# An order written out for every engine is replaced by another, with twelve small dummy matmuls near its start

## The chip, the cores and the metric

One core of one Trainium2 chip runs the kernel. Five engines work side by side on that core, each through its own list of instructions in order: TensorE (PE, matmuls), VectorE (DVE), ScalarE (ACT), GpSimd (POOL) and SyncE (SP, which here only issues transfers). The metric is device microseconds (us) of one execution.

## What is computed

Attention whose mask comes from hashes, then a channel mix with squared relu. Cut to its core, with batch 4, 8 heads, 768 positions and head size 64:

```
bucket(x) = sum_k 2**k * ((x @ proj)[k] > 0)                  # 6 bits
mask      = bucket(q)[:, None] == bucket(k)[None, :]
attn      = softmax(where(mask, q @ k.T / 8, -1e9))           # per batch and head
x         = attn @ v, heads side by side                      # 4 x 768 x 512
xk, xr    = mu_k*x + (1-mu_k)*x_prev, mu_r*x + (1-mu_r)*x_prev # x_prev: one position back
out       = sigmoid(xr @ w_r) * (relu(xk @ w_k)**2 @ w_v)      # d_ff 1024
```

## The kernel before

The heads are worked two at a time: 16 pairs, n = 0 to 15, four pairs to a batch. Each pair goes through a chain of steps; the names are those that the planner's keys use, with the line that issues them.

- Loads (`ldq`, `ldv`, L452 to L470, SP) bring q, k and v of a pair. `hi` (L540, for pairs 0 to 2 L612 and L614) and `lo` (L543, L617; DVE) split q and k into two halves of 16 bits.
- Transposes: for pairs 0 to 2 by PE (`t`, L631) with a copy out (`evt`, L635, DVE or ACT), for the rest by a DMA (`tr`, SP). A step ends in a digit that stands for the head of the pair: `lo0q1` is pair 0, q, head 1.
- Hash bits: 24 small matmuls (`bits`, L571), one DVE step (`bx`, L575) and two or four small DMAs (`row`, L595, SP) write the bits as extra rows beside q and k, so that the score matmul adds the mask. For pair 0 the bits go straight (`b`, L653, and `beb`, L659 on ACT or L661 on DVE).
- Scores: nine steps for each pair, 1024 columns each, `sc` (L704, PE) then `exp` (L708, ACT). A score step takes two PSUM banks of six (banks 0 to 5, slots 0, 2, 4) and holds them until its `exp` has read them.
- Values: `va`, `vsum`, `vsumb`, `vsumc` (L485 to L499, POOL or DVE), `oo` (L732, L737, PE), `rc` and `ob` (L747 to L754, DVE), `ot` and `xt` (L790 to L796) or a DMA transpose, `xs` and `xj` (L772 to L777, a small shift).
- After the four pairs of a batch, the channel mix of that batch: `df`, `xk`, `xr` (DVE), 16 steps `kp` (L855, PE) with `relu` (L860 on ACT, L862 on DVE) and a squaring `sq` (L865, DVE), and six steps each of `r` (L880, PE), `tanh` (L883, ACT), `v` (L895, PE), `os` (L902, DVE) and a store (L906). The channel mix of one batch lies among the scores of the next; the last one has nothing behind it.

Nothing of the order is decided when the kernel is built. `add` and `add_on` collect about 1400 steps. Three tables say the rest: `WHERE` gives an engine to each step that has a choice, `SLOT` a PSUM bank to each matmul step, and `ORDER` is the sequence in which `schedule` hands the steps out. Each engine works off its own steps in that sequence, and a step that waits holds up all that stand behind it on its engine. The dummy matmuls on a zeroed buffer (`warm`, L370, seven of 128x512) take part in the order as any other step; a second set (L373) stands in the code with a count of 0. The weights come by DMA and are cast by the steps `wc` (L434 to L436).

Of the kernel before, what the change touches and what calls it, by code (L numbers as in the profile page):

```python
# [36 lines left out]
def R(kind, n):  # L37
# [195 lines left out]
def kernel(  # L233
# [13 lines left out]
    nc = tc.nc  # L247
# [5 lines left out]
    P = 128  # L253
# [11 lines left out]
    NWARM2 = 0  # L265
# [90 lines left out]
    def sm(name):  # L356
        b_ = plan.slot[name]
        return ps_all[:, b_ * 512 : (b_ + 1) * 512]
# [604 lines left out]
```

## Time and profile before

| | |
|---|---|
| median of three runs | 250.05 us (248.19, 250.05, 250.88) |
| the profiled execution | 248.25 us, of which 246.5 us is the span from its first instruction to its last |
| outside the span | 1.75 us |
| granted TensorE clock | 1.000 |
| PE instructions | 2643 matmuls, 2643 weight loads |

A line of the profile's groups reads: line, engine, operation, what it writes and reads, shapes, count, then busy us and mean ns of one, then the idle time of the engine before such instructions and what ended it. In the sequences a number behind a line is its start in us from the span's begin and the next its length. The length of a matmul has its way through the array in it; from one matmul's start to the next is the time that it takes of PE.

### The profile page before, as it was taken

What the parts mean: (1) busy time and instruction counts of PE and PEld (TensorE: products, weight loads), DVE (VectorE), ACT (ScalarE), POOL (GpSimd) and SP (SyncE); (2) the same over time, 40 slices, a digit from 0 to 9 for tenths busy, and PEclk for the clock granted to TensorE, in tenths of its full rate; (3) what the DMA queues carried; (4) which work ended last, traced back from release to release, by engine and by line L of the source; (5) the groups of instructions that cost most, each with busy time, mean ns of one, the idle gap of its engine ahead of it and who ended that gap; (6) DMA issues with size and microseconds to landing.
All of it is one profiled execution on the core that took longest, in us unless ns stands there. A gap on an engine that the chain in (4) does not pass through costs nothing.

```text
span 246.5 us, 6589 instructions
## 1 busy us (share of the span) xinstructions
PE 236.3 (96%) x2643; PEld 148.2 (60%) x2643; DVE 193.7 (79%) x451; ACT 178.0 (72%) x224; POOL 52.5 (21%) x104
## 2 busy tenths in 40 slices
PE   6989899999999999999999999999999999999994
PEld 2456578876766656556566567755676554455443
DVE  3899977879999797879999788889569986575313
ACT  3698979999999988669878999998873241334320
POOL 5132841348114221204221113013010000000000
PEclk9999999999999999999999999999999999999999
DMA  6986998899689899996989797695211031321033
GB/s 188 338 289 180 199 274 172 299 225 164 195 272 236 277 187 292 215 264 176 220 277 176 207 292 150 171 199 126 88 32 47 12 107 43 128 86 44 0 128 128
DMA packets 71161, 43.77 MB, mean 178 GB/s; under 512 B 51356, under 2 KB 66140, under 8 KB 71132
## 3 DMA queue, kind: packets, MB, share of 16 engines
q1 hardware_dynamic: 71036, 43.36, 69.7%
q8 instruction: 20, 0.33, 0.5%
q14 instruction: 9, 0.07, 0.1%
q10 hardware_dynamic: 96, 0.01, 0.0%
HBM read 24.12 MB, written 6.29 MB: 123 GB/s over the span
## 4 chain that ended last, share of the span: by engine, by line
PE 76%; DVE 14%; DMA 5%; issue 2%; SPq 1%; ACT 1%; POOL 0%; DVEq 0%
PE ps_all L704 19%; PE ps_all L895 16%; PE ps_all L855 15%; PE ps_all L737 10%; PE ps_all L880 8%; PE ps_all L571 4%; DMA a<-bx 4%; DVE nh L543 3%; DVE nh L540 2%; DVE nh L617 1%; DMA pj<-in_proj_dram 1%; DVE ob L754 1%; SPq L595 1%; DVE a L661 1%; PE ps_all L631 1%
## 5 line engine op out<-in xcount | busy, mean ns | idle before, releaser
L708 ACT ACTIVATE pt<-ps_all 128x1024 bf16<-128x1024 f32 x144 | 138.2, 1044 | 14.6 <-PE ps_all L704 13.3
L704 PE MATMUL ps_all<-a 128*128 128x256 f16 (+3 forms) x408 | 80.4, 316 | 0.9 <-DMA a<-bx 0.8
L855 PE MATMUL ps_all<-xk,wk 128*128 128x384 bf16 x256 | 49.5, 326 | 0.0
L737 PEld LDWEIGHTS <-pt 128*128 128x128 bf16 x1152 | 43.1, 97 | 9.2 <-issue 1.1
L704 PEld LDWEIGHTS <-a 128*128 128x128 f16 x408 | 34.9, 97 | 22.4 <-issue 2.6
L895 PE MATMUL ps_all<-wv,k 128*128 128x512 bf16 (+2 forms) x208 | 46.5, 362 | 0.5 <-DVE ob L754 0.5
L737 PE MATMUL ps_all<-va,pt 128*128 128x65 bf16 x1152 | 45.2, 193 | 0.0
L855 PEld LDWEIGHTS <-wk 128*128 128x128 bf16 x256 | 24.1, 98 | 16.1 <-issue 0.8
L860 ACT ACTIVATE kr<-ps_all 128x384 bf16<-128x384 f32 x37 | 17.7, 494 | 20.3 <-PE ps_all L855 13.5
L895 PEld LDWEIGHTS <-k 128*128 128x128 bf16 x208 | 19.5, 98 | 19.8 <-issue 0.8
L883 ACT ACTIVATE rs<-ps_all 128x512 f32<-128x512 f32 x24 | 14.1, 598 | 22.1 <-PE ps_all L880 17.7
L902 DVE SCALAR_TENSOR_TENSOR os<-rs,ps_all 128x512 f32<-128x512 f32 (+2 forms) x26 | 16.7, 643 | 15.9 <-PE ps_all L895 9.1
L865 DVE TENSOR_TENSOR k<-kr 128x384 bf16<-128x384 bf16 x64 | 23.6, 387 | 5.0 <-ACT kr L860 4.8
L543 DVE SCALAR_TENSOR_TENSOR nh<-nat,nh 128x768 f16<-128x768 f32 x26 | 25.9, 1005 | 0.6 <-issue 0.2
L880 PE MATMUL ps_all<-wr,xr 128*128 128x512 bf16 x96 | 23.7, 379 | 0.0
L862 DVE TENSOR_SCALAR kr<-ps_all 128x384 bf16<-128x384 f32 x27 | 14.9, 552 | 6.8 <-PE ps_all L855 6.1
L754 DVE TENSOR_TENSOR ob<-ps_all,rc 128x384 bf16<-128x384 f32 (+1 forms) x36 | 18.1, 508 | 1.3 <-DMA xt<-ob 0.7
L540 DVE TENSOR_SCALAR nh<-nat 128x768 f16<-128x768 f32 x22 | 15.1, 689 | 0.3 <-DMA nat<-in_k_dram 0.2
L880 PEld LDWEIGHTS <-xr 128*128 128x128 bf16 x96 | 9.0, 98 | 9.5 <-issue 0.2
L571 PE MATMUL ps_all<-a,p0g 128*32 128x256 f16 (+1 forms) x180 | 12.9, 276 | 0.1
L571 PE MATMUL ps_all<-a,p1g 128*32 128x256 f16 (+1 forms) x180 | 12.8, 273 | 0.0
L485 POOL CAST va<-vn 128x768 bf16<-128x768 f32 x7 | 7.7, 1096 | 22.4 <-DMA vn<-in_v_dram 20.8
(93 smaller groups left out, 210.9 us busy)
## 6 DMA issues: line engine op xcount, KB each, us to landing
vn<-in_v_dram SPq DMA_DIRECT2D x16, 384.0 KB
out_dram<-os SPq DMA_DIRECT2D x23, 256.0 KB
nat<-in_q_dram SPq DMA_DIRECT2D x15, 384.0 KB
nat<-in_k_dram SPq DMA_DIRECT2D x15, 384.0 KB
wst<-in_moe_w_k_dram SPq DMA_DIRECT2D x2, 512.0 KB
wst<-in_moe_w_r_dram SPq DMA_DIRECT2D x2, 512.0 KB
wst<-in_moe_w_v_dram SPq DMA_DIRECT2D x2, 512.0 KB
a<-bx SPq DMA_DIRECT2D x48, 9.0 KB
```

The source lines that it names most:

```text
L540: e.tensor_scalar(out=o, in0=x, scalar1=QS, scalar2=None, op0=ALU.mult)
L543: nc.vector.scalar_tensor_tensor(out=nh[:, :, D:P], in0=nat.rearrange("p j (c d) -> p (j c) d", d=D), scalar=QS, in1=nh[:, :, 0:D], op0=AL ...
L571: nc.tensor.matmul(ps[g_ * wid : (g_ + 1) * wid, 0:FW], w_[:, m_ - 1 - x : m_ - 1 - x + wid], a_t[sa][:, i, x % NFOLD * FW : (x % NFOLD + ...
L704: nc.tensor.matmul(ps[:, lo - s * w : hi - s * w], side_a["k"][sa][:, j, jc * P : (jc + 1) * P], side_a["q"][sa][:, j, q0 : q0 + hi - lo], ...
L708: nc.scalar.activation(out=pt_t[sp][:, s * w : (s + 1) * w], in_=ps_all[:, plan.slot[nm] * 512 : plan.slot[nm] * 512 + w], func=AF.Exp, bi ...
L737: nc.tensor.matmul(oo[:, (ic - c0) * 65 : (ic - c0) * 65 + 65], pt_t[sp][:, o : o + P], va_t[sa][:, j, jc, 0 : D + 1], start=(not uc and i ...
L754: nc.vector.tensor_tensor(out=ob_t[so][:, c0:c1, j * D : (j + 1) * D], in0=oo[:, :, 0:D], in1=rc_t[sr][:, 1, c0:c1].unsqueeze(2).to_broadc ...
L855: nc.tensor.matmul(ps[:, 0:HALF], wk_sb[:, d, fc * P : (fc + 1) * P], xk_t[mx[d]][:, h * HALF : (h + 1) * HALF], start=(d == 0), stop=(d = ...
L860: nc.scalar.activation(out=kr_t[sk], in_=sm(nm)[:, 0:HALF], func=AF.Relu, scale=0.5 ** 0.5)
L865: nc.vector.tensor_tensor(out=k2_t[s2][:, h * HALF : (h + 1) * HALF], in0=kr_t[sk], in1=kr_t[sk], op=ALU.mult)
L880: nc.tensor.matmul(sm(nr), xr_t[mx[d]][:, c * P : (c + 1) * P], wr_sb[:, d, :], start=(d == 0), stop=(d == NDC - 1))
L895: nc.tensor.matmul(sm(nv)[:, lo:hi], k2_t[(b * NFC + fc) % NK2][:, c * P : (c + 1) * P], wv_sb[:, fc, lo:hi], start=(fc == 0), stop=(fc == ...
```

## The change

Twelve dummy matmuls of 128x256 (`keep`, L373) are added beside the seven `warm`, and all three tables are new. The dummies have places in the order as all other steps have.

```
-    NWARM2 = 0
+    NKEEP = 12
...
-    for i in range(NWARM2):
-        add("PE", 0.2155, -7.5 + 0.15 * i, lambda: nc.tensor.matmul(sm("warm2"), wz[:, 0:P], wz, start=True, stop=True),
...
+    for i in range(NKEEP):
+        add("PE", 0.109, -7.5 + 0.15 * i, lambda: nc.tensor.matmul(sm("warm2")[:, 0:256], wz[:, 0:P], wz[:, 0:256], start=True, stop=True),
...
 WHERE = {
-    "wc8": "ACT", "wc9": "POOL", "hi0q0": "DVE", "evt0q00": "DVE", ...
+    "wc8": "POOL", "wc9": "DVE", "hi0q0": "DVE", "evt0q00": "ACT", ...
 SLOT = {
-    "warm": 7, "mu": 6, "t0q00": 7, "b0q00": 7, "t0q01": 6, ...
+    "warm": 6, "warm2": 7, "mu": 6, "t0q00": 4, "b0q00": 6, "t0q01": 5, ...
 ORDER = [
...
+    0, 76, 84, 85, 79, 77, 110, 111, 9, 10, 11, 2, 3, 4, 104, 5, 12, 13, 27, 51, 78, 82, 105, 6,
...
```

What changes engine, counted over the new table: nine `relu` go from ACT to DVE in sum (37 on ACT and 27 on DVE become 28 and 36; by batch, ACT has 6, 9, 10, 12 before and 6, 5, 12, 5 after); three `vsum` steps go from POOL to DVE; of 18 `xs`, POOL has 14 before and 6 after (DVE 9, ACT 3); three `xj` go from POOL to DVE; one weight cast goes from ACT to POOL and one from POOL to DVE; one `beb` goes from DVE to ACT; of 14 copies `evt`, ACT has 5 before and 3 after. SP issues the same transfers, in another order.

What the new sequence is at the start, by names and engine (before above, after below):

```
PE   warm*4 t0k10 warm*3 t0q10 b0k10 t0k01 b0q10 t0q01 t0k00 t0q00 b0k01 sc0_5 b0q00 t1q10 b0k00 sc0_7 ...
     keep*3 warm*4 keep*2 warm keep*2 warm t0q01 keep*2 t0q00 keep t0k10 keep warm t0q10 keep b0k10 b0q10 t0k01 b0q00 t1k00 sc0_8 sc0_7 t0k00 b0q01 b0k01 sc0_6 ...
PE   ... bits2 sc1_4 sc1_2 oo0_0*2 sc1_7 sc1_6 oo0_1*2 sc1_0 oo0_0 sc1_1 oo0_1 sc2_1 sc2_7 ot0 sc2_5 mu sc2_6 bits3
     ... bits2 sc1_4 sc1_1 oo0_0 sc1_0 mu oo0_0*2 sc1_6 sc1_7 oo0_1*2 sc1_2 oo0_1 sc2_3 sc2_7 sc2_5 ot0 sc2_1 bits3
DVE  hi0k1 lo0k1 hi0q1 lo0q1 hi0k0 lo0k0 evt0q10 hi0q0 lo0q0 beb0q10 evt0q00 hi1q1 ...
     hi0q0 lo0q0 hi0k1 lo0k1 hi0q1 lo0q1 evt0k10 hi0k0 evt0q10 lo0k0 lo1k0 beb0q10 evt0q01 ...
DVE  ... evt2k10 vsum0 vsum0b hi4k bx2 hi3k lo3 lo4 hi4q lo4 rc0 ob0 rc0 ob0 muv xt0_0
     ... evt2k00 bx2 hi3k lo3 lo4 muv rc0 hi5q hi4k ob0 rc0 ob0 lo4 xt0_0
ACT  ... exp1_4 exp1_2 exp1_7 exp1_6 exp1_0 exp1_1 exp2_1 exp2_7 exp2_6
     ... exp1_4 exp1_1 exp1_0 exp1_6 exp1_7 exp1_2 exp2_3 exp2_5 exp2_7
SP   ldq0k1 ldq0q1 ldq0k0 ldq0q0 ldq1q ldq1k ldq2q ldq2k ldv1 ...
     ldq0q0 ldq0k1 ldq0q1 ldq0k0 ldq1k ldq2q ldq1q ldq2k ldq3q ldv0 ...
```

`mu` is a small matmul that turns the two mix vectors; `muv` is its DVE copy.

More of the change, by code (lines that the diff above doesn't have):

```diff
@@ L371 @@
             r=["wz"], w=["warm"], take=("sm", "warm", 0) if i == 0 else None, give=["warm"] if i == NWARM - 1 else [], name="warm")
-    for i in range(NWARM2):
-        add("PE", 0.2155, -7.5 + 0.15 * i, lambda: nc.tensor.matmul(sm("warm2"), wz[:, 0:P], wz, start=True, stop=True),
-            r=["wz"], w=["warm2"], take=("sm", "warm2", 0) if i == 0 else None, give=["warm2"] if i == NWARM2 - 1 else [], name="keep")
+    for i in range(NKEEP):
+        add("PE", 0.109, -7.5 + 0.15 * i, lambda: nc.tensor.matmul(sm("warm2")[:, 0:256], wz[:, 0:P], wz[:, 0:256], start=True, stop=True),
+            r=["wz"], w=["warm2"], take=("sm", "warm2", 0) if i == 0 else None, give=["warm2"] if i == NKEEP - 1 else [], name="keep")
     add("ACT", 1.5, -9.5, lambda: nc.scalar.activation(out=tb[:, 0:1], in_=tb[:, 1:2], func=AF.Exp), r=["tb"], w=["tb0"], at=0.75, name="table")
```

227 rows, old and new, of tables (ORDER, SLOT, WHERE) are left out of this document.

## The prediction

> **What bounds the kernel now.** I read the page first (busy shares, then the slices), then busy time by stages, then the waits of PE, then the start in order of time on PE, DVE and ACT, because the slices show that PE is short of work only there.
>
> ```profile
> span 246.5 us, 6589 instructions
> PE 236.3 (96%) x2643; PEld 148.2 (60%) x2643; DVE 193.7 (79%) x451; ACT 178.0 (72%) x224; POOL 52.5 (21%) x104
> PE   6989899999999999999999999999999999999994
> DVE  3899977879999797879999788889569986575313
> ACT  3698979999999988669878999998873241334320
> ...
> L708 ACT ACTIVATE pt<-ps_all 128x1024 bf16<-128x1024 f32 x144 | 138.2, 1044 | 14.6 <-PE ps_all L704 13.3
> ...
> L860 ACT ACTIVATE kr<-ps_all 128x384 bf16<-128x384 f32 x37 | 17.7, 494 | 20.3 <-PE ps_all L855 13.5
> ...
> L862 DVE TENSOR_SCALAR kr<-ps_all 128x384 bf16<-128x384 f32 x27 | 14.9, 552 | 6.8 <-PE ps_all L855 6.1
> ...
> L540 DVE TENSOR_SCALAR nh<-nat 128x768 f16<-128x768 f32 x22 | 15.1, 689 | 0.3 <-DMA nat<-in_k_dram 0.2
> ```
> ```profile
> 0.00:32.00 32.00, 27.05 (x275) 16.40 (x275) 25.47 (x48) 24.65 (x32) 13.69 (x43) 1.00 0.85 238
> 32.00:66.00 34.00, 33.34 (x582) 25.67 (x582) 28.95 (x67) 32.57 (x36) 15.30 (x24) 1.00 0.92 224
> 66.00:131.00 65.00, 63.80 (x710) 39.43 (x709) 57.43 (x131) 54.94 (x66) 14.79 (x21) 1.00 0.96 237
> 131.00:186.00 55.00, 55.00 (x708) 35.93 (x709) 44.70 (x116) 48.12 (x57) 8.74 (x16) 1.00 0.73 158
> 186.00:246.50 60.50, 57.17 (x379) 30.79 (x375) 37.18 (x92) 17.71 (x36) 0.00 (x0) 1.00 0.21 73
> ```
>
> The columns after the stretch's length are PE, weight loads, DVE, ACT, POOL, then clock, DMA share and GB/s. PE idles 4.95 us to 32, 0.66 to 66, 1.20 to 131, none to 186, and 3.33 behind its last matmul: 10.14 us. A matmul's length runs into the next, so short gaps are hidden and this is a lower bound. From 32 to 66 ACT is the tight one (32.57 of 34): there is no channel mix yet to fill PE, and the scores wait for their exponentials. From 66 on PE is the bound. So a new order can gain in three places only: the start, ACT's saturation up to 66, and 1.2 us of waits up to 131.
>
> **The start, and its prices.**
>
> ```profile
> PE ps_all L631 <- POOL p L391: 1.2, 1, 1.2
> ...
> PE ps_all L790 <- DVE ob L754: 1.0, 1, 1.0
> PE ps_all L704 <- DMA a<-bx: 0.8, 2, 0.5
> ...
> PE ps_all L895 <- DVE ob L754: 0.5, 1, 0.5
> ```
> ```profile
> 1.19 1.89 PE L370 MATMUL ps_all<-k 128*128 128x512 bf16 x4 [1.19 <-DVE k L367]
> 4.28 0.82 PE L631 MATMUL ps_all<-idh,nh 128*128 128x128 f16 x6 [1.20 <-POOL p L391]
> 4.89 1.49 PE L370 MATMUL ps_all<-k 128*128 128x512 bf16 x3
> 6.17 0.85 PE L631 MATMUL ps_all<-idh,nh 128*128 128x128 f16 x6
> ...
> 11.40 0.51 PE L631 MATMUL ps_all<-idh,nh 128*128 128x128 f16 x6
> ...
> 23.42 1.04 PE L704 MATMUL ps_all<-a 128*128 128x512 f16 x5
> ...
> 29.04 1.05 PE L704 MATMUL ps_all<-a 128*128 128x128 f16 x8 [0.32 <-DMA a<-bx]
> 31.08 0.51 PE L790 MATMUL ps_all<-idb,ob 128*128 128x128 bf16 x6 [1.00 <-DVE ob L754]
> ```
> ```profile
> 3.27 0.36 DVE L614 TENSOR_SCALAR nh<-nat 128x384 f16<-128x384 f32 x1 [2.13 <-DMA nat<-in_k_dram]
> 3.66 0.56 DVE L617 SCALAR_TENSOR_TENSOR nh<-nat,nh 128x384 f16<-128x384 f32 x1
> ...
> 5.91 0.36 DVE L614 TENSOR_SCALAR nh<-nat 128x384 f16<-128x384 f32 x1 [0.83 <-DMA nat<-in_k_dram]
> ...
> 7.06 0.56 DVE L635 COPY a<-ps_all 128x768 f16<-128x768 f16 x1 [0.19 <-PE ps_all L631]
> ...
> 9.13 0.95 DVE L661 TENSOR_SCALAR a<-ps_all 6x768 uint16<-6x768 uint16 x1 [0.66 <-PE ps_all L653]
> ```
> ```profile
> 18.79 0.42 DVE L575 TENSOR_SCALAR bx<-ps_all 128x256 uint16<-128x256 uint16 x1
> ...
> 23.53 0.42 DVE L575 TENSOR_SCALAR bx<-ps_all 128x256 uint16<-128x256 uint16 x1 [0.32 <-PE ps_all L571]
> ...
> 26.93 1.17 DVE L540 TENSOR_SCALAR nh<-nat 128x768 f16<-128x768 f32 x1
> ...
> 32.92 0.55 DVE L540 TENSOR_SCALAR nh<-nat 128x768 f16<-128x768 f32 x1
> ```
> ```profile
> 10.99 1.02 ACT L708 ACTIVATE pt<-ps_all 128x1024 bf16<-128x1024 f32 x1
> ```
> ```profile
> 24.07 7.62 ACT L708 ACTIVATE pt<-ps_all 128x1024 bf16<-128x1024 f32 x8 [0.57 <-PE ps_all L704]
> 32.92 1.94 ACT L708 ACTIVATE pt<-ps_all 128x1024 bf16<-128x1024 f32 x2 [1.24 <-PE ps_all L704]
> ```
>
> **The dummies.** Three 128x512 dummies fill 4.89 to 6.17: 0.427 us each, although the clock column says 1.00; six transposes at 6.17 take 0.85 us, at 11.40 they take 0.51. So the array is slow early and quick later. A 256-column dummy is 0.213 us at the slow pace. Ahead of the first transposes the new order has seven dummies of 256 and six of 512: 7 x 0.213 + 6 x 0.427 = 4.05 us from 1.19, so to 5.24 at most. The first transposes can start when the first load has landed (3.27) and `hi` and `lo` are through (4.22): up to 1.0 us late. Their reader is `evt0q00`, which no step wants soon; the step that matters is `evt0k10`, which stands on DVE behind `lo0q1`, whose load is now third. The third load lands at 5.91 in the DVE rows, so `lo0q1` ends at 6.86 and PE is long free. I take 0. Bounds: the dummies uncovered cost 12 x 0.213 = 2.6 us; a quick clock from 5 us on saves at most half of the slow PE work up to about 8 us, some 1.3.
>
> The Trainium skill (TensorE: Matmul & The Clock Gate, Part 1) says that the array starts at half rate and is released after some 3.4 us of activity, and that this ramp should be modelled as under 1% of a kernel. The pace halving between 6.17 and 11.40 agrees; by it the dummies bring no more than the 1.3 us just bounded, and the sum stands.
>
> **The first exponential.** On DVE the new order runs from 6.86: `evt0k10` 0.56, `hi0k0` 0.36, `evt0q10` 0.56, `lo0k0` and `lo1k0` 0.56 each, `beb0q10` 0.95, to 10.4. Before, 0.9 us pass from the end of that `beb` (9.13 and 0.95) to the first `exp` at 10.99, with other work between; with 0.6 to 0.9 it now starts at 11.0 to 11.3. I take zero; one us sooner if the third load lands nearer to the second, which was there by 4.2.
>
> **Pairs 1 and 2.** `sc1_4` (23.42) follows `bx1` (18.79) by 4.6 us and `sc2_1` (29.04) follows `bx2` (23.53) by 5.5. Up to `bx1` DVE has about one 0.56 us step more in the new order: the exponentials of pair 1 start some 0.4 late, at 24.5. `bx2` now stands right behind the last `evt2`, with nothing to do while PE makes the 24 hash matmuls (about 1.4 us): `bx2` comes at 24.9 by my count, 1.4 late, so pair 2's first scores at 29.5 to 30.4. Six exponentials of pair 1 (0.95 each from 24.5) cover until 30.2. What is won stands behind that: before, `ot0` waits 1.00 us on PE for `ob0` at 31.08 with `sc2_5` and `sc2_6` behind it, and ACT idles 1.24 us until 32.92. The new order puts `sc2_5` ahead of `ot0`, so three exponentials run without a break. ACT's third exponential of pair 2 starts at 32.0 to 32.9 instead of 32.92. I take -0.7. As ACT is full from there to 66, this is carried to the end.
>
> **POOL and DVE.** The same `hi` takes 1.17 us at 26.93 and 0.55 at 32.92. Its mean over 22 is 0.689, so what lies over 0.55 sums to 22 x 0.14 = 3.1 us of DVE in the whole run. The change gives DVE nine more `relu` (9 x 0.552 = 5.0 us) and takes 9 x 0.494 = 4.4 from ACT; the small steps that leave POOL add below 2 us to DVE. The Trainium skill (GPSIMD Engine Reference, 8 Key points) states that GpSimd shares its SBUF interfaces with VectorE and contends with its two-input and two-port instructions. No row here names the cause of the 1.17; if it is that, fewer POOL steps win back a part of the 3.1 us, which is less than the 5.0 added.
>
> **The middle.** Up to 131 PE has 1.2 us of visible waits, such as 0.5 on `ob` and 0.5 for a hash row. In the new order the distance from hash bits to first scores is as short as before, about 4.6 to 6 us of PE work, so such waits come and go. ACT has four `relu` less (2.0 us). I take -0.5, bounds +3.2 (second rival) and -1.2.
>
> **The tail.** From 131 to 186 PE has no idle, and behind that only its own work. DVE gets 7 more `relu` of batch 3 (3.9 us) on 37.18 of 60.5: room. The last steps are the same. 0.
>
> Sum: 0 + 0 - 0.7 - 0.5 = -1.2 us. The profiled execution took 248.25 (span 246.5 and 1.75 around); the median of three is 250.05, 1.80 above. On the median that gives 248.9, on the profiled one 247.1.
>
> **Rivals.** *Faster.* The waits at the start go altogether: the third load lands with the second (-1.0), both ACT waits (0.57 and 1.24) vanish (-1.8), and most of the middle's 1.2 with them (-0.8): -3.6, 246.4. For it: ACT's idle to 32 is 7.35 us, and all of it is carried. Against it: `bx2` without filler ahead.
>
> *Slower: DVE paces the channel mix.* From 66 to 131 DVE does 57.43 of 65, 88%. Four more `relu` (2.2) and some small shifts (0.7) make 60.3. If it cannot be filled better than 88%, since each step waits for PE or ACT first, the stage lasts 60.3/0.884 = 68.2: +3.2, so 253.3. It decides once DVE needs over 93% of that stage. Against it: several slices of that stage show a 9, so 90% and more is reached.
>
> *The change does not do what it says.* The dummies delay `t0q01` by the 1.0 us and the delay reaches the first `exp`, with no other gain: 251.0.
>
> **Chances.** The forecast 0.32, the delay 0.10, faster 0.33, slower 0.25. A measurement of this kernel can tell about 1% from no change (its three runs spread over 2.7 us), so under 247.5 is faster and over 252.6 slower: faster 0.33, same 0.42, slower 0.25. The range for 8 in 10 goes from 245.0 (the faster rival and some more of PE's idle) to 254.0 (the slower rival and some); the likeliest case alone spans 247 to 251.
>
> **What would show it.** Dummies: six transposes at the start take about 0.51, and `t0q01` starts near 5. First exponential at about 11.0; pair 1's at 24.5; no ACT wait near 32, but a DVE wait of over 1 us at the second `bx`. ACT at 95% or more from 33 to 65. DVE above 60 us in the stage to 131 with PE's idle there not above 1.2 (the slower rival: above 3). Stages behind 131 without PE idle. Wrong would be: a changed tail, a late load that holds the start, or new waits for hash rows.

## The result, and the profile after

| | before | after |
|---|---|---|
| median of the runs | 249.87 us | 253.16 us (251.10 to 254.71) |
| ratio, with its interval | | 1.0126 [1.0077, 1.0176] |
| the profiled execution | 248.25 us, span 246.5 | 251.10 us, span 249.3 |

The changed kernel is slower. In two later jobs, each beside the kernel before, the ratio was 1.011 [1.0075, 1.0146] and 1.0084 [1.0043, 1.0124]. The forecast was 248.9 us. The time lies inside the range of 245 to 254, but the forecast was a small gain and the result a loss of 2 to 3 us.

First the page of the changed kernel, the lines that answer to those of before.

```profile
span 249.3 us, 6618 instructions
PE 237.1 (95%) x2655; PEld 149.3 (60%) x2655; DVE 195.2 (78%) x472; ACT 173.8 (70%) x217; POOL 44.4 (18%) x90
PE   7878999989999999999999999899999999999993
DVE  3997788777969899779989798686688879769423
ACT  2697999989999878993958899898882333202211
...
L860 ACT ACTIVATE kr<-ps_all 128x384 bf16<-128x384 f32 x28 | 13.5, 493 | 17.2 <-DVE k L865 11.3
...
L862 DVE TENSOR_SCALAR kr<-ps_all 128x384 bf16<-128x384 f32 x36 | 19.6, 553 | 6.4 <-PE ps_all L855 5.0
...
L540 DVE TENSOR_SCALAR nh<-nat 128x768 f16<-128x768 f32 x22 | 12.2, 565 | 1.2 <-DMA nat<-in_k_dram 0.9
```

Busy time by stages (after the length: PE, weight loads, DVE, ACT, POOL, then clock, DMA share, GB/s):

```profile
0.00:32.00 32.00, 27.60 (x288) 17.60 (x289) 24.77 (x49) 23.06 (x31) 11.77 (x46) 1.00 0.84 229
32.00:66.00 34.00, 32.57 (x556) 24.70 (x554) 27.46 (x78) 33.08 (x37) 11.02 (x13) 1.00 1.10 232
66.00:131.00 65.00, 64.03 (x740) 39.97 (x739) 56.59 (x126) 52.76 (x64) 16.97 (x22) 1.00 1.01 237
131.00:186.00 55.00, 53.47 (x627) 33.83 (x626) 44.69 (x117) 48.36 (x57) 4.67 (x9) 1.00 0.77 160
```

PE's idle time by stages, 4.95, 0.66, 1.20 and 0 before, is now 4.40, 1.43, 0.97 and 1.53. The 0.55 less at the start is no gain: the dummies count as busy time there. The stage that had none, 131 to 186, has 1.53. The DMA share has risen in the two stages from 32 to 131, from 0.92 to 1.10 and from 0.96 to 1.01, with nearly the same GB/s; from 131 to 160 alone it is 0.99 (0.94 before). (A share of 1.10 can only be if packets overlap in this count, so 1 isn't a hard limit of it; "full" means a share near 1 in what follows.)

What PE waits for, in the changed kernel (total us, times, longest):

```profile
PE ps_all L631 <- DVE nh L617: 1.7, 2, 0.9
PE ps_all L704 <- DMA a<-bx: 1.6, 4, 0.7
PE ps_all L571 <- DMA a<-nh: 1.6, 2, 1.3
```

Before, hash rows (`a<-bx`) cost 0.8 us and the transposes of q and k (`a<-nh`) were not among the waits shown. The places, in PE's order of time; the bracket is the idle time before the row and what ended it:

```profile
50.66 1.04 PE L704 MATMUL ps_all<-a 128*128 128x512 f16 x5 [0.75 <-DMA a<-bx]
...
69.58 0.61 PE L704 MATMUL ps_all<-a 128*128 128x512 f16 x2 [0.49 <-DMA a<-bx]
```
```profile
133.99 0.59 PE L704 MATMUL ps_all<-a 128*128 128x512 f16 x2 [0.19 <-DMA a<-bx]
...
156.93 0.29 PE L571 MATMUL ps_all<-a,p0g 128*32 128x256 f16 x4 [1.34 <-DMA a<-nh]
```

The last of them can be followed into SP's own queue:

```profile
144.07 2.20 SPq L764 DMA_TRANSPOSE xt<-ob  x1
146.32 0.58 SPq L465 DMA_DIRECT2D nat<-in_k_dram  x1
146.95 0.46 SPq L465 DMA_DIRECT2D nat<-in_q_dram  x1
147.51 2.37 SPq L595 DMA_DIRECT2D a<-bx  x3
149.99 3.36 SPq L547 DMA_TRANSPOSE a<-nh  x2
```

SP issues without a break in this stretch. The transposes that `bits14` reads are issued from 149.99 to 153.35 and PE gets them at 156.93. One DMA transpose holds SP for 1.7 to 2.2 us here, one row transfer for 0.8 (2.37 for three), so what stands ahead of a late transfer on SP delays it by as much. Over a longer stretch SP does pause, for it waits in its own order until a source is ready:

```profile
92.75 0.92 SPq L431 DMA_DIRECT2D wst<-in_moe_w_v_dram  x2
95.64 2.37 SPq L595 DMA_DIRECT2D a<-bx  x3
```

From 66 to 160 us the lengths of its issues come to 81.8 of 94 us in the changed kernel and 80.0 before.

And the DMA queue of the page (packets, MB, share of 16 engines), after and then before:

```profile
q1 hardware_dynamic: 71036, 43.36, 73.6%
```
```profile
q1 hardware_dynamic: 71036, 43.36, 69.7%
```

The same 71036 packets took 0.736 x 249.3 = 183.5 us of all engines in place of 0.697 x 246.5 = 171.8.

### The profile page after: what moved, and what is told of

It is laid out like the page before. It is cut to its first block, busy times and chain, and to the rows that moved or that the text cites. A ratio compares the mean times of both kernels' runs of the same rounds, so it can differ in the third digit from the quotient of the medians.

```text
span 249.3 us, 6618 instructions
## 1 busy us (share of the span) xinstructions
PE 237.1 (95%) x2655; PEld 149.3 (60%) x2655; DVE 195.2 (78%) x472; ACT 173.8 (70%) x217; POOL 44.4 (18%) x90
## 3 DMA queue, kind: packets, MB, share of 16 engines
q1 hardware_dynamic: 71036, 43.36, 73.6%
## 4 chain that ended last, share of the span: by engine, by line
PE 75%; DMA 12%; DVE 6%; SPq 3%; issue 1%; ACT 1%; DVEq 0%
PE ps_all L704 19%; PE ps_all L895 16%; PE ps_all L855 14%; PE ps_all L737 11%; PE ps_all L880 8%; DMA a<-bx 8%; PE ps_all L571 4%; DMA nat<-in_k_dram 2%; DMA a<-nh 2%; SPq L595 2%; DVE nh L617 1%; PE ps_all L732 1%; SPq L465 1%; DVE a L635 1%; PE ps_all L631 1%
## 5 line engine op out<-in xcount | busy, mean ns | idle before, releaser
L855 PE MATMUL ps_all<-xk,wk 128*128 128x384 bf16 x256 | 50.2, 326 | 0.5 <-DVE kr L862 0.5
L860 ACT ACTIVATE kr<-ps_all 128x384 bf16<-128x384 f32 x28 | 13.5, 493 | 17.2 <-DVE k L865 11.3
L865 DVE TENSOR_TENSOR k<-kr 128x384 bf16<-128x384 bf16 x64 | 23.1, 374 | 3.1 <-ACT kr L860 2.7
L543 DVE SCALAR_TENSOR_TENSOR nh<-nat,nh 128x768 f16<-128x768 f32 x26 | 25.2, 974 | 0.3
L862 DVE TENSOR_SCALAR kr<-ps_all 128x384 bf16<-128x384 f32 x36 | 19.6, 553 | 6.4 <-PE ps_all L855 5.0
L540 DVE TENSOR_SCALAR nh<-nat 128x768 f16<-128x768 f32 x22 | 12.2, 565 | 1.2 <-DMA nat<-in_k_dram 0.9
L575 DVE TENSOR_SCALAR bx<-ps_all 128x256 uint16<-128x256 uint16 x15 | 6.3, 422 | 8.5 <-PE ps_all L571 7.3
```

Source lines behind the costliest of these rows:

```text
L543: nc.vector.scalar_tensor_tensor(out=nh[:, :, D:P], in0=nat.rearrange("p j (c d) -> p (j c) d", d=D), scalar=QS, in1=nh[:, :, 0:D], op0=AL ...
L855: nc.tensor.matmul(ps[:, 0:HALF], wk_sb[:, d, fc * P : (fc + 1) * P], xk_t[mx[d]][:, h * HALF : (h + 1) * HALF], start=(d == 0), stop=(d = ...
L862: nc.vector.tensor_scalar(out=kr_t[sk], in0=sm(nm)[:, 0:HALF], scalar1=0.5 ** 0.5, scalar2=0.0, op0=ALU.mult, op1=ALU.max)
L865: nc.vector.tensor_tensor(out=k2_t[s2][:, h * HALF : (h + 1) * HALF], in0=kr_t[sk], in1=kr_t[sk], op=ALU.mult)
```

## The experiments

Four theories stand against one another. A: SP's new sequence is bad, and a better sequence for the same work mends it. B: the dummies lie on the path, 1.3 us of PE. R (E in some of the texts): the new order of the engines' work loses behind some 50 us because its hash transfers come late, and as SP and the DMA engines have little room there, each wait goes through to the end at its full price. The fourth is the slower rival of the prediction, DVE; the stage table refutes it without a run: DVE has 56.59 us from 66 to 131, less than the 57.43 before, and not over 60. The texts also name C, F and T; each says what it means.

### Which part of the change: dummies, start, rest

`e1`: the changed kernel without the dummies, all other steps in their sequence. `e2`: the kernel before with the twelve dummies put among its seven.

```
e1   -    NKEEP = 12
     +    NKEEP = 0
e2   PE   warm*4 +keep*7 t0k10 warm*3 +keep t0q10 +keep b0k10 +keep t0k01 +keep b0q10 +keep t0q01 ...
```

> The changed kernel without its twelve dummies, every other step in the same sequence. Theory A (the new order of SP's transfers lets hash rows and DMA transposes reach PE late, some 3 us of waits): the start waits for loads and DVE anyway, so the time stays within 0.6 us of the changed kernel, about 253. Theory B (the dummies lie on the path: PE is the bound from 66 us on, and 12 x 0.109 = 1.3 us of work was added): 1.3 us faster, about 251.8, up to 2.6 if they run at the slow pace. Theory C (the new sequences of PE, DVE and ACT are worse by themselves): within 0.6.

Measured: 251.38 us, ratio 1.0054 [1.0023, 1.0084]. This is what B said, not A.

> The kernel before with the same twelve dummies put among its first PE steps: seven ahead of the first transposes and one ahead of each of the next five PE steps; nothing else moved. Theory A: within 0.6 us of before. Theory B: 1.3 to 2.6 us slower than before. Theory C: within 0.6. If the quicker clock is worth anything at the start, up to 0.7 faster.

Measured: 249.83 us, ratio 0.9998 [0.9969, 1.0027]. The dummies cost the kernel before nothing and bring it nothing: its first `exp` came at 10.14 in place of 10.99, the lead of 0.7 us lasted to pair 5, and by the end of pair 7 other waits had used it up.

`c1` is the changed kernel once more. `s1` takes the new order's first 424 steps and the old order for the rest; `s2` the old order's first 427 steps and the new order for the rest, without dummies; `s3` the new order's first 900 steps (in the traces DVE and ACT part from the new order near 140 us, SP near 133) and then the old one. Engines and banks of each step go with the part that it is taken from.

> The changed kernel once more, unaltered, timed beside the two splices so that they are read against the same runs, and beside the version without dummies (251.4). If the dummies lie on the path, it is again near 253.2, 1.3 us or more above that version; if they are covered, it comes out at 251 to 252.

Measured: 252.84 us, 1.011 [1.0075, 1.0146].

> A splice: the new order (with its engines, banks and dummies) for the first 424 steps, to about 62 us, and the order of before for all that is left. Theory E (the new order loses behind 131 us, where the hash transfers of pairs 11 to 14 reach PE late by 2 us): as before or better, 249 to 250. Theory F (it loses up to 66: dummies and a start that ends later): as the changed kernel, 252 to 253.

Measured: 251.89 us, 1.0078 [1.0046, 1.011].

> The counterpart: the order of before for the first 427 steps, to about 62 us, then the new one; no dummies. Theory E: as the changed kernel, 252 to 253. Theory F: as before, 250.

Measured: 253.34 us, 1.0135 [1.0105, 1.0165].

> The new order for the first 900 steps, to about 140 us, then the order of before. Theory E: as before, 249.5 to 250.5, if the loss lies behind the joint; if it lies between 62 us and the joint, 252 to 253 here and 250 in the splice at 62. Theory F: 252 to 253 in both.

Measured: 255.18 us, 1.0187 [1.0145, 1.0229].

`s2` tells most: the old start with the new rest, and not one dummy, is as slow as the whole change. This points to the rest, but does not show it. `s1` and `s3` are slower than before too, and both miss what E said of them (249 to 250 and 249.5 to 250.5); `s3` misses F as well. A joint of two orders costs something itself: `s3` waits 4.0 us for hash rows, more than either parent, and in `s2` PE waits 1.02 us for `kr` at 77.71, soon behind the joint, where neither parent does. So the splices place nothing by themselves; `h2`, below, places the loss behind 66 us without a joint. Of the new start `s1` and `s3` only say that it brings no gain that outlives it.

### Is it SP's sequence?

`e3` gives the new order SP's old sequence, from its 31st transfer on (but for one pair of transposes that must follow two others). `e5` puts each pair's row transfers together and as early as their sequence allows, and moves loads and one output transpose behind them. `f2` does this for the rows alone, `f1` for pair 11 alone; `f3` is `f2` without dummies. All other engines keep their sequences.

```
f1   -SP  ... ldq13k row11 row11 ldq14k row11 ldv11 ldq13q row11 tr12 ...
     +SP  ... ldq13k row11 row11 row11 row11 ldq14k ldv11 ldq13q tr12 ...
e5   -SP  ... row12 row12 ldv13 row12 row12 otd9 ldq15k ldq15q row13 row13 row13 tr14 tr14 row13 ...
     +SP  ... row12 row12 row12 row12 ldv13 row13 row13 row13 row13 otd9 tr14 tr14 ldq15k ldq15q ...
```

> The changed kernel with SP's sequence of transfers, from the 31st on, as in the kernel before (but for one pair of transposes that must follow two others). PE, DVE, ACT, POOL and the dummies as in the changed kernel. Theory A: most of the 3.2 us comes back: 250 to 251, with the wait at the hash bits of pair 14 (1.3 us) gone. Theory B: no change, about 253. Theory C: no change or slower, since the sequence was made for other orders.

Measured: 285.01 us, 1.1374 [1.1312, 1.1435]. The granted clock stood at 0.5 for 17 us of its profiled execution, so up to 8.5 us of the loss come from that. Its waits, in PE's table:

```profile
PE ps_all L571 <- DVE os L902: 7.0, 1, 7.0
PE ps_all L704 <- DMA a<-bx: 5.7, 2, 2.9
PE ps_all L732 <- DVE kr L862: 4.2, 1, 4.2
```

> The changed kernel with SP's sequence mended at the places where its trace shows waits: the rows of a pair stand together behind their first one, and a weight load, a v load, a DMA transpose of the result (pair 9) and two loads (pair 15) go behind the hash transfers that they stood ahead of. Theory A: the waits on hash rows and on transposes in the PE list (1.6 and 1.6 us) fall below 1 us in sum, and the time by 2 to 3 us, to 250 to 251. Theory B and C: within 0.6 us of 253.

Measured: 261.44 us, 1.0458 [1.0409, 1.0507]. The waits for rows fell to 0.5 us, and this came instead:

```profile
PE ps_all L855 <- DVE kr L862: 5.7, 2, 5.0
```

DVE works in its own fixed sequence; up to 160 us it stood 4.90 us behind a load of q that now came late, and PE behind DVE.

> The changed kernel; on SP the four hash rows of pair 11 go one behind the other, so the last of them no longer stands behind three loads. Nothing else moves. Five profiled runs of this order showed PE waiting there for a hash row: 0.19, 2.77, 1.71, 1.06 and 1.95 us, 1.54 in the mean. Theory R (those waits, in stages where PE has no other slack, reach the end at full price): 1.5 us faster, about 251.4, and no wait for a row of pair 11. Rival T (any transfer moved on SP brings its own wait, as the first mending did): no gain or slower.

Measured: 252.88 us, 1.0076 [1.004, 1.0113], not to be told from the changed kernel's 1.0084 to 1.0126.

> The changed kernel; the hash rows of every pair go one behind the other, from the place of the first. No load, weight load or DMA transpose is moved behind anything but those rows (the first mending had also moved five of them far back). Theory R: all waits for rows go but those for transposes: 2 to 2.5 us faster, about 250.5. Rival T: no gain or slower; where it is slower, a load or a transpose that now stands behind rows shows as the wait.

Measured: 255.23 us, 1.0195 [1.0152, 1.0239].

> As the version with all rows together, and without the twelve dummies. If the dummies cost their 12 x 0.109 = 1.3 us in this order, it is 1.3 us below that version; if they are covered, within 0.6.

Measured: 257.62 us, 1.024 [1.0181, 1.0299]. Most of its executions ran with a dip of the granted clock, so nothing on the dummies is read from it.

In `f1` the wait of pair 11's scores for their rows is gone. On DVE, and then on PE, the trace shows what took its place:

```profile
134.47 0.56 DVE L493 TENSOR_TENSOR vt<-vn 128x384 f32<-128x384 f32 x1 [0.52 <-DMA vn<-in_v_dram]
...
136.01 0.56 DVE L540 TENSOR_SCALAR nh<-nat 128x768 f16<-128x768 f32 x1 [0.98 <-DMA nat<-in_q_dram]
```
```profile
138.82 0.29 PE L571 MATMUL ps_all<-a,p0g 128*32 128x256 f16 x4 [1.18 <-DVE kr L862]
```

The rows moved ahead of three loads; two of these came late, DVE waited 0.52 + 0.98, and `bits12` waits 1.18 us three to four us later. The same in `f2`, where the waits of the hash matmuls for transposes rose from two to four and from 1.6 to 4.9 us:

```profile
PE ps_all L571 <- DMA a<-nh: 4.9, 4, 1.9
PE ps_all L855 <- DVE kr L862: 2.5, 2, 1.7
```

So theory A falls in this form: every sequence of SP that was tried moves the wait or adds to it. The reverse test is `f4`: the kernel before, with one transpose put ahead of pair 11's last row.

```
f4   -SP  ... row11 row11 ldq13k row11 tr12 tr12 tr13 ...
     +SP  ... row11 row11 ldq13k tr12 row11 tr12 tr13 ...
```

> The kernel before; one DMA transpose (of pair 12, some 1.5 to 1.9 us of SP) goes ahead of the last hash row of pair 11, nothing else moves. Theory R: PE waits there 1.5 to 2 us longer, in a stage where it has no slack, and the end comes as much later: 251.5 to 252. Rival T or any slack behind: less than 0.6.

Measured: 252.8 us, 1.0086 [1.0053, 1.0118], 2.1 us above the kernel before in that job.

```profile
133.70 0.60 PE L704 MATMUL ps_all<-a 128*128 128x512 f16 x2 [1.68 <-DMA a<-bx]
```

One place swapped in a sequence of 177 transfers makes the kernel before nearly as slow as the changed one: a wait of 1.68 us in the middle arrives at the end whole. The two traces bear this out. The 90th of the 144 exponentials ends 1.15 us later than in the kernel before (the two starts differ by more than that already at the first pair), the 108th, which lies behind the swap, 2.75 later, and the last instruction 2.8: the swap adds 1.6, and nothing wins it back.

### Is it the load of the DMA engines?

SP's issue time and the DMA engines' load go together in all of these. `g1` and `g2` part them: each load of q, k and v from pair 3 on brings one head instead of two, in the changed kernel and in the kernel before; SP issues as many transfers, in the same sequence. (The second head of these pairs is computed from what its buffer holds, so that part of the output is not right.) `h1` is `g1` once more; `h2` lightens the loads from pair 8 on only.

```
+            h_ = 1 if n > 2 else 2
...
-                              in_=v[b, 2 * t : 2 * t + 2].rearrange("j (p c) d -> p j (c d)", c=NSC))
+                              in_=v[b, 2 * t : 2 * t + h_].rearrange("j (p c) d -> p j (c d)", c=NSC))
```

> The changed kernel, in which the q, k and v loads of pairs 3 to 15 bring only the first of their two heads (192 KB in place of 384 KB in each of 39 transfers, 7.5 MB of the 43.8 MB; the second head is computed from what its buffer holds, so this part of the output is left out). Every engine's instructions, SP's too, stay in number and order. If the waits of the new order come from the load of the DMA engines (mean share 1.01 from 66 to 131 us), they go: the rows of TensorE at L704 and L571 that wait for a<-bx and a<-nh fall from 1.6 us each to under 0.6 us, and the time falls by 2 us or more, to 251 us or below against 253.2. If they come from SP's issue time, or from the order in which SP issues, the waits stay over 1 us each and the time within 1 us of 253.2.

Measured: 249.67 us, 0.997 [0.9933, 1.0007].

> The kernel before with the same lighter loads (the second head of pairs 3 to 15 left out). It is the yardstick for the changed kernel with lighter loads: if the load of the DMA engines makes the difference between the two orders, the difference is gone or turned with light loads, the changed kernel then 0 to 1.2 us ahead (its lead at the end of pair 3). If the orders alone make it, the changed kernel stays 2 to 3.5 us behind. By the first theory the kernel before gains little itself, under 1.5 us, since its rows waited 0.8 us in all.

Measured: 249.95 us, 1.0002 [0.9972, 1.0032].

> The changed kernel without its twelve dummy matmuls (1.31 us of TensorE), a second time and beside the changed kernel itself in the same job. If the dummies lie on the path, it is 1.0 to 1.4 us faster than the changed kernel here; if other work covers them, within 0.6 us of it.

Measured: 252.65 us, 1.0106 [1.007, 1.0143].

> The changed kernel as it is, a third time, as the yardstick for the one without dummies and for those with light loads. It should stand 2.5 to 3.3 us behind the kernel before.

Measured: 252.95 us, 1.0084 [1.0043, 1.0124].

> The changed kernel with the lighter loads of pairs 3 to 15 once more (the second head of those pairs left out), for a profile in which the granted clock does not dip: the first profile of it had a dip to 0.7 between 12 and 19 us. If the DMA engines' load makes the waits, the rows of TensorE that wait for a<-bx and a<-nh sum to under 1.5 us here (3.2 us in the changed kernel's profile, 4.4 in its third), and the time is again 249.0 to 250.3 us. If the first measurement misled, the waits sum to over 3 us and the time is over 251.5.

Measured: 249.32 us, 0.9948 [0.9913, 0.9983].

> The changed kernel with lighter loads for pairs 8 to 15 only (their second head left out): the transfers up to some 60 us stay as heavy as they were, those behind are lighter. By the account of TensorE's time the new order loses 0.7 us from 40 to 66 us and 2.0 us from 131 to 160 us: then most of what the lighter loads win must stay, 249.7 to 250.9 us. If the loss came from the waits at 41 to 70 us, little of it is won and the time stays at 251.8 us or over.

Measured: 249.29 us, 0.9969 [0.9941, 0.9996].

With lighter loads the kernel before stays where it was and the changed kernel falls by 3.3 to 3.6 us, to the same time or a little below: the loss is there only under the full load of the DMA engines. Every engine keeps the changed kernel's sequence in these runs, so C, by which the new sequences are worse by themselves, is out. `h2` places the loss: the load that counts is that from pair 8 on, whose first light transfer is issued at 66.38 us in its trace; what is lightened ahead of that brings nothing more. The stages of the changed kernel's third profile (`g4`), then of `h2`:

```profile
66.00:131.00 65.00, 62.73 (x728) 39.15 (x733) 55.38 (x125) 53.29 (x64) 15.94 (x22) 1.00 0.98 233
131.00:186.00 55.00, 53.99 (x627) 34.22 (x630) 45.34 (x118) 47.48 (x55) 4.67 (x9) 1.00 0.80 165
```
```profile
66.00:131.00 65.00, 64.31 (x743) 40.27 (x742) 58.34 (x128) 53.13 (x65) 16.64 (x22) 1.00 0.85 196
131.00:186.00 55.00, 54.23 (x637) 34.33 (x635) 44.70 (x117) 48.83 (x58) 4.69 (x9) 1.00 0.67 123
```

PE's idle time from 66 to 186 is 2.27 + 1.01 = 3.28 us in the one and 0.69 + 0.77 = 1.46 in the other, and 1.20 in the kernel before. Some 0.5 of the 3.28 are gaps of 0.05 us, most of them where the trace lacks a matmul's record. The two executions took 251.84 and 250.34 us, 1.50 apart, so the idle time accounts for about that. The waits for transfers fell only in part. The waits table of `h1`, in which two expected rows were to come to under 1.5 us:

```profile
PE ps_all L580 <- DMA a<-nh: 1.0, 2, 0.7
PE ps_all L713 <- DMA a<-bx: 0.6, 1, 0.6
```

They come to 1.6 (the lines are nine higher by the added code). `g1` had 2.4, not the under 0.6 each that was expected, and `h2` 2.9, of which 1.85 stand before its loads get light; the profiles of `g1` and `h1` hold a dip of the granted clock in the first stage. In the five profiles of the new order at full load with SP's sequence unaltered (the changed kernel, `c1`, `g4`, and without dummies `e1` and `g3`) these rows come to 3.2, 6.0, 4.4, 3.5 and 4.2. By place, the wait for a row of pair 11, near 137 us, is in all five (0.2, 2.8, 0.8, 1.7 and 0.3) and in none of the three with light loads; there only the wait of `bits14` is left behind 75 us, 0.7 in each. From `c1` and from `h2`:

```profile
139.74 0.59 PE L704 MATMUL ps_all<-a 128*128 128x512 f16 x2 [2.77 <-DMA a<-bx]
```
```profile
155.98 0.29 PE L580 MATMUL ps_all<-a,p0g 128*32 128x256 f16 x4 [0.69 <-DMA a<-nh]
```

The times are clear, and the waits fit them; that these waits and nothing else make up the 3 us is not shown.

One more thing that the lighter load changes can be read at the transposes, in their lines of the changed kernel and of `h2` (least, median and longest time in ns that one holds SP, then the starts of the first and the last in us):

```profile
L547 SPq DMA_TRANSPOSE a<-nh x26: 1402/1920/3472, 22.7 to 163.9; - x26
```
```profile
L556 SPq DMA_TRANSPOSE a<-nh x26: 1361/1838/3160, 22.6 to 163.0; - x26
```

From 66 to 160 us alone the mean is 2.09 us in the changed kernel and 2.02 in `g4`, 1.82 in `h2` and 1.71 in `h1`, 14 of them each; in the kernel before it is 1.93, and 1.75 in `g2`. So SP's time is not apart from the load: 14 x 0.29 = 4 us of SP in that stretch, and the light loads do not part the two causes wholly. The order counts too, for `f4` has 1.82 at full load. What it is that the transpose waits for, these rows do not tell.

The dummies stay unsettled. `e1` was 1.4 to 1.8 us below the changed kernel measured in other jobs, `g3` only 0.3 below `g4` in its own, and `e2` showed nothing. B as the main cause is out, since `s2` is slow without dummies and the light loads are quick with them; a part of it, some 1 us by the mean of `e1` and `g3`, can be true.

No version that computes everything was faster than the kernel before.

## Why the prediction was wrong, step by step

**What failed: "The middle" and "The tail".** The prediction took -0.5 there since waits for hash rows "come and go" with the distance between hash bits and scores as short as before, and 0 behind 131, since PE had no idle there. It looked at the distance in PE's order alone. The transfers between have to pass SP, which spends 87% of the time from 66 to 160 us on issuing, and DMA engines at a share of 0.99 to 1.01; a new order of PE's steps shifts each transfer's due time, and every attempt to bring one forward delayed another (`f1`, `f2`, `e5`). An estimate by the starts of PE's matmuls, each counted with its usual cost and the dummies left out, finds the changed order level up to 40 us, 0.7 to 1.0 behind at 66, 0.2 to 0.6 behind at 131 and 2.2 to 2.4 behind at 160; with 0.5 more until the last output lands that is the 2.8 us between the two profiled executions. In the sum, -0.5 and 0 should have been +2 to +3. That the time lies inside the range is luck: its upper end and the bound of +3.2 were priced for DVE, and DVE was not the cause. The falsifier that the prediction named, "new waits for hash rows", is what came.

**The start: the gain came, and by the clock it won nothing.** Three excerpts of the changed kernel, of PE, DVE and ACT:

```profile
4.55 0.33 PE L631 MATMUL ps_all<-idh,nh 128*128 128x128 f16 x3
...
7.46 1.50 PE L653 MATMUL ps_all<-a,p 128*32 128x512 f16 x8
...
9.59 0.51 PE L631 MATMUL ps_all<-idh,nh 128*128 128x128 f16 x6
```
```profile
9.40 0.96 DVE L661 TENSOR_SCALAR a<-ps_all 6x768 uint16<-6x768 uint16 x1
...
24.67 0.42 DVE L575 TENSOR_SCALAR bx<-ps_all 128x256 uint16<-128x256 uint16 x1 [1.56 <-PE ps_all L571]
```
```profile
11.65 2.87 ACT L708 ACTIVATE pt<-ps_all 128x1024 bf16<-128x1024 f32 x3
...
25.21 11.46 ACT L708 ACTIVATE pt<-ps_all 128x1024 bf16<-128x1024 f32 x12 [0.29 <-PE ps_all L704]
```

`beb0q10` ends at 10.36, counted 10.4. The first `exp` starts at 11.65, not at 11.0 to 11.3: ACT has two copies and two `hi` steps between, and 1.3 us pass where 0.6 to 0.9 were counted; in the other profiles of the new order it lies anywhere from 10.8 to 12.1, as the first loads land sooner or later, and of the old one from 10.1 to 12.1. Pair 1 starts at 25.21 (24.5 forecast), `bx2` at 24.67 (24.9 counted) behind the foretold wait of over 1 us, and the ACT wait near 32 is gone: twelve exponentials run without a break. From the first `exp` to the end of the 36th, pair 3's last, the kernel before takes 39.6 us and the changed one 38.9: the -0.7 that was taken. But the later first `exp` uses it up, and the 36th ends at 50.58 and 50.56. (Other profiles of the old order have 39.8 to 40.6 for this stretch, of the new one at full load 38.5 to 39.0, but for `e3` and `g3`, so the gain may be nearer to 1.3; where a profile's first `exp` falls differs by more than that.) It is right behind this that ACT stops again: pair 4's scores wait at 50.66 for their row. So the remark that the gain "is carried to the end" because ACT is full to 66 was wrong.

**The dummies** stay within their bounds: `t0q01` starts at 4.55 (near 5 was said). What they win is uncertain. Eight matmuls of L653 take 1.50 us here; without dummies they took 1.58 in `e1`, and as much in `f3`, but 2.31 in `g3`:

```profile
7.01 1.58 PE L653 MATMUL ps_all<-a,p 128*32 128x512 f16 x8
```
```profile
7.74 2.31 PE L653 MATMUL ps_all<-a,p 128*32 128x512 f16 x8
```

So the array was at full pace by then in two of three profiles without dummies, and 0.8 us of work later in the third, within the 1.3 that bounded this. Nothing of it reached the end, as `e2` shows.

**POOL and DVE.** The nine `relu` moved as counted (28 on ACT, 36 on DVE). The mean `hi` (L540) fell from 689 to 565 ns, which is 22 x 0.124 = 2.7 us of the 3.1 that the prediction put over its quick time, with POOL's busy time down from 52.5 to 44.4. So DVE's sum rose by 1.5 us only, and the slower rival lacked its ground; the prediction's own sign, DVE above 60 us in the stage to 131, failed as well (56.59). The traces bear on the slow `hi`: before, nine of the 22 ran with nothing on POOL and took 0.56 us or less, and the seven above 0.56, up to 1.36, all ran beside a POOL instruction; in the changed kernel only two ran beside one, and one of these is the only slow one (0.85). Six before ran beside POOL and were quick, so it is not every POOL instruction. The contention that the Trainium skill (GPSIMD Engine Reference, 8 Key points) names fits this; no run here changes POOL alone.

**ACT** had 33.08 of 34 us from 32 to 66 (97%, forecast 95% or more).

## What to carry to other kernels

Where one queue issues every transfer with few breaks and the DMA engines are full, a new order of the compute engines is a new set of due times for transfers, and its price is to be sought in that queue: for each transfer the time when its source is ready, what stands ahead of it, and who waits. A gain at the start is not carried by the engine that is full behind it if that engine's next input hangs on such a transfer. To tell order from load, lighten the load in both versions and leave the order: if the difference goes, the load was needed for it. A gain between two marks in a trace is none until the second mark itself comes earlier.

## What the runs showed of the hardware that was not expected

- The same packets took 171.8 us of all DMA engines in one order and 183.5 in the other. The packets of 256 bytes, which the transposes make, took 77.3 and 84.6 us of this for 48384 packets, those of 1536 bytes 53.8 and 57.6. This sum does not measure the loss: `s2`, as slow as the changed kernel, had 171.4.
- SP's sequence alone, under the same sequences of all other engines, moved the changed kernel from 253 to 285 us (`e3`), part of it by dips of the granted clock.
- The granted clock can dip to 0.5 of full speed for 3.4 us (at 16.0 us in `g1`'s profile, 16.3 in `g3`'s, 16.5 in `h1`'s; where 0.7 is said above, it is the mean of a longer slice). By the mean clock, at most 0.993, it did so in 16 of the 48 executions with light loads and in 2 of 54 of the kernel before beside them, but also in 6 of the 20 of `g3` and `g4` at full load, so the light load is not what it takes. In `g1`, `g2` and `h1` the medians of executions with a dip lie 1.3 to 2.9 us above those without.
